# First block of a convolution and SiLU kernel: 32 by 32 tiles of TensorE for the convolution, and a new order of the work around it

## The chip, the cores and the metric

The kernel runs on one core of one Trainium2 chip. Five engines work side by side, each with its own queue in program order: TensorE (PE in the profile; its weight loads are PEld), VectorE (DVE), ScalarE (ACT), GpSimd (POOL) and SyncE (SP), which issues most DMAs. The metric is the device time of one execution in microseconds, the median of several runs; lower is better.

## The reference

```python
def _attn_ref(x, weight):            # x: (8, 4096, 192), weight: (8, 7)
    w = exp(weight - max(weight)) ; w = w / (sum(w) + 1e-9)      # per head, over the 7 taps
    x_pad = concatenate([zeros(6 tokens), x])                    # causal, per sequence
    out[b, s, c] = sum over k of w[head of c, k] * x_pad[b, s + k, c]

def _moe_ref(x, w_in, w_out):        # x: 32768 tokens x 192; w_in: 192 x 2048; w_out: 2048 x 192
    h = x @ w_in
    return (h * (1 / (1 + exp(-h)))) @ w_out
```

A head has 24 channels, so neighbouring channels share their seven taps. `w_in` and `w_out` arrive as 64-bit floats; x, the taps and the result are 32-bit.

## The kernel before, in words

The 32768 tokens go in 32 blocks of 1024 (`TT`), in two halves of 512 (`TB`). Blocks 1 to 31 follow a long list of tokens (`PLAN`): there x and `w_in` are split into parts that TensorE multiplies in a faster format, with products saved by sums of weights. Block 0 is written out by hand, because everything that the others need must first be made: taps, the 64-bit weights turned into 32 bits, and their split parts. The change touches only block 0 and what stands ahead of it.

**Layout.** x has 192 channels. Channels 0 to 127 stand in `nats[0]` (tokens in partitions, 32 at a time) and after a transpose in `xts[0]` (channels in partitions, six columns of `pad` ahead for the causal halo). Channels 128 to 191 stand in `nats[1]` and `xts[1]`, tokens 0 to 511 in partitions 0 to 63 and tokens 512 to 1023 in partitions 64 to 127. After the convolution the same memory is called `x_first[0]` and `x_first[1]`.

**Start** (lines 206 to 247, 390 to 421). SyncE and ScalarE issue the loads: the logits `wexp`, the first half of x in four DMAs, the first part of `w_in` for j=0, the second half of x, channels 128 to 191 (`load(0, 4..7)`), then the other parts of `w_in`. GpSimd makes `sel` (which head a channel belongs to) and `one_hot`. The softmax of the taps runs on VectorE and ScalarE with 8 partitions, and `spread_taps` multiplies it by `sel` on TensorE so that every channel has its taps. `heat` is a matmul of zeros.

**Convolution of block 0.** For channels 0 to 127, `conv_on_pe` (650) multiplies on TensorE with seven diagonal matrices `diags` of 128 by 128, made by ScalarE (line 695), into one PSUM bank for each half of the tokens; `conv_taken` copies a bank to `x_first[0]`. For channels 128 to 191, `conv` (438) runs seven steps on `xts[1]`: the first on ScalarE, six on VectorE.

**Weights.** `Unit` 2j and 2j+1 turn the two parts of column group j of `w_in` (rows 0 to 127 and rows 128 to 191) into 32-bit floats in `wd`. `exponent` is one VectorE and two GpSimd operations, `sign` one on ScalarE, `mantissa`, `sticky` and `rounded` five on VectorE; `top` is the first split part, on ScalarE; `spread` moves rows of the second part to the other half of the partitions by two DMAs. `work(u)` (615) is a generator in two pieces: the first also begins unit u+1, the second rounds, takes the top part and spreads. Units 8 to 11 do `w_out`.

**First products.** `up_first(j, c0)` (675) computes h for column group j, two chunks c of 128 columns and both token halves: four PSUM banks, four products over 128 channels (`x_first[0]`) and four over 64 (`x_first[1]`), then four SiLUs on ScalarE. Banks are taken from and given back to the list `homes`, which has eight. `woven` (637) lays the pieces of two lists into one program order: the next piece is always from the list whose summed cost so far is the smaller share of its whole. One list is the weights (`rest`, whole 392), the other the first products (whole 432). This order holds on each engine; ScalarE does SiLUs, top parts, signs and split parts from the one queue.

After that block 0 multiplies by `w_out` (`down_plain`), and block 1 begins. `halo_in` (423) brings the last six tokens of one block ahead of the next.

Of the kernel before, what the change touches and what calls it, by code (L numbers as in the profile page):

```python
# [18 lines left out]
def kernel(  # L19
# [166 lines left out]
    nats = [const.tile([P, n, SQ], F32, name=f"nat{i}") for i, n in enumerate((TT // SQ, TB // SQ))]  # L186
    xts = [const.tile([P, pad + n], F32, name=f"xt{i}") for i, n in enumerate((TT, TB))]
    xs = [const.tile([P, 3, n], F32R, name=f"xs{i}") for i, n in enumerate((TT, TB))]
# [16 lines left out]

    HALVES = [slice(0, TB // SQ), slice(TB // SQ, TT // SQ)]
    wexp = const.tile([H, K], F32, name="wexp")
    sync.dma_start(out=wexp, in_=weight)
    for i in (1, 0, 2, 3):
        load(0, i, act if i == 1 else sync, HALVES[0])  # L210

# [5 lines left out]

    sel = const.tile([H, 2, P], F32, name="sel")
    one_hot = g_all[:, 0, 1, 0, 0:P]
    vec.memset(one_hot, 0.0)  # L220
    pool.memset(sel, 1.0)
    for sign, base in ((1, 0), (-1, grp - 1)):
        for view, pattern, first in (
            (sel[:, 0, :], [[sign, P]], 0),
            (sel[:, 1, :].rearrange("p (a c) -> p a c", a=2), [[0, 2], [sign, R]], P),
        ):
            pool.affine_select(
                out=view,
                in_=view,
                compare_op=ALU.is_ge,  # L230
                fill=0.0,
                base=base + sign * first,
                pattern=pattern,
                channel_multiplier=-sign * grp,
            )
    pool.affine_select(
        out=one_hot,
        in_=one_hot,
        compare_op=ALU.not_equal,
        fill=1.0,  # L240
        base=0,
        pattern=[[-1, P]],
        channel_multiplier=1,
    )
    pool.memset(xts[0][:, 0:pad], 0.0)
    pool.memset(xts[1][0:R, 0:pad], 0.0)
# [46 lines left out]
    class Unit:  # L293


        def __init__(self, index, key, part):
            j = key[1]
            self.key, self.part, self.j = key, part, j
            lo, hi = {0: (0, CA), 1: (CA, WC), None: (0, WC)}[part]
# [19 lines left out]
        def exponent(self):  # L319
            vec.tensor_single_scalar(self.ex, self.hi, 0x7FF * ONE, op=ALU.bitwise_and)  # L320
            pool.tensor_scalar(
                self.ex, self.ex, scalar1=float(896 * ONE), scalar2=float(1151 * ONE), op0=ALU.max, op1=ALU.min
            )
            pool.tensor_scalar(
                self.ex, self.ex, scalar1=float(896 * ONE), scalar2=8.0, op0=ALU.subtract, op1=ALU.mult
            )
# [51 lines left out]
    def heat(times):  # L378
        for _ in range(times):
            pin(  # L380
                nc.tensor.matmul(
                    banks[7][:, 0 : 2 * P],
                    zeros,
                    zeros.unsqueeze(1).to_broadcast([P, 2, P]),
                    start=True,
                    stop=True,
                )
            )
# [8 lines left out]
    wred = const.tile([H, 3], F32, name="wred")  # L397
# [4 lines left out]
    act.activation(warm, warm, AF.Silu)  # L402
    vec.tensor_scalar(total, total, scalar1=1e-9, scalar2=None, op0=ALU.add)
    vec.reciprocal(part_, total)
    vec.tensor_scalar(wexp, wexp, scalar1=part_, scalar2=None, op0=ALU.mult)

    def spread_taps(k):
        to = banks[6][:, K * k : K * k + K]
        pin(nc.tensor.matmul(to, sel[:, k, :], wexp, start=True, stop=True))

    def take_taps(k):
        vec.tensor_copy(taps[:, k, :], banks[6][:, K * k : K * k + K])

    spread_taps(0)
    heat(1)
    take_taps(0)

    def turn_in(b, k, cols=slice(0, None)):
        vec.transpose(xts[k][:, pad:][:, cols], flat(nats[k])[:, cols])

    turn_in(0, 0, slice(0, TB))
# [193 lines left out]
    def work(u):  # L615

        now = units[u]
        if u:
            begin(u + 1)
        now.mantissa()  # L620
        now.sticky()
        if 2 * NJ < u + 1 < len(units):
            units[u + 1].sign()
        yield
        if not u:
            begin(1)
        now.rounded()
        if u == 1:
            conv_taken(1)
        if now.part is not None:  # L630
            now.top()
# [15 lines left out]

    diags = flat(g_all[:, 0, 6])[:, 0 : K * P].rearrange("p (i c) -> p i c", c=P)

    def conv_on_pe(n):  # L650
        for i in range(K):
            mm(banks[n], diags[:, i, :], xts[0][:, n * TB + i : n * TB + i + TB], i == 0)
            if n == i == 0:
                spread_taps(1)
        homes.append(homes.pop(0))

    def conv_taken(n):
        act.copy(x_first[0][:, ts(n, TB)], banks[n])

# [44 lines left out]
    next(first_[0])  # L704
    turn_in(0, 1)
# [105 lines left out]
```

## Time and profile before

| | |
|---|---|
| median of 3 runs | 2232.61 us (2232.59 to 2232.68) |
| the profiled execution | 2231.81 us, its span 2230.1 us |
| busy in the span | PE 2220.2, DVE 1823.2, ACT 1289.9, POOL 60.9 us |
| products of block 0 by `w_in` | from 18.14 to 62.78 us |
| product of block 0 by `w_out` | 41.4 us from 62.78 us |

Rows of a timeline are: start and length in us, engine, line, operation, what is written and read, partitions by elements and their type, how many are merged (x7), and in brackets the idle time before them and what ended it. L142 and L461 are helpers through which most instructions go, so rows are told apart by the names: `ps` is PSUM, `nat`, `xt`, `g`, `wd`, `w_a`, `w_b`, `fin` and `taps` are the tiles above. A 32-bit matmul shows as two records. 128*128 ahead of the shape is rows by columns of the array that are in use. In groups, the numbers are total busy us, mean ns of one, and idle us before them.

### The profile page before, as it was taken

The numbers are of one execution on the slowest core, as the hardware profiler recorded it, in microseconds if no ns is written. First come the engines' busy times: TensorE is split into PE (matmuls) and PEld (weight loads), VectorE is DVE, ScalarE is ACT, GpSimd is POOL, SyncE is SP. The second block draws the span as 40 slices with busy tenths as digits, with TensorE's granted clock in tenths as the row PEclk, the third lists the DMA queues.
The fourth block names the chain that finished last, engine by engine and source line by source line (L and its number), as shares of the span: only waits on it lengthen the run. The fifth ranks groups of instructions, "written<-read, shape, count | busy, mean of one in ns | idle before, by whom it ended". The sixth has DMA issues, their size and how long they took to land.

```text
span 2230.1 us, 46938 instructions
## 1 busy us (share of the span) xinstructions
PE 2220.2 (100%) x19208; PEld 1638.6 (73%) x19208; DVE 1823.2 (82%) x3017; ACT 1289.9 (58%) x2646; POOL 60.9 (3%) x74
## 2 busy tenths in 40 slices
PE   9999999999999999999999999999999999999998
PEld 4377777777777777777777777777777777777776
DVE  8797888877888878888778887788887788877867
ACT  5266655567555676555665556765466654567543
POOL 6300000000000000000000000000000000000000
PEclk9999999999999999999999999999999999999999
DMA  6301011111011110111110111101111001111001
GB/s 147 61 16 30 11 20 30 30 30 24 7 30 30 30 29 8 23 30 30 30 20 11 29 30 30 30 8 23 30 30 30 16 14 30 30 30 30 5 12 30
DMA packets 408105, 61.75 MB, mean 28 GB/s; under 512 B 402257, under 2 KB 406353, under 8 KB 407889
## 3 DMA queue, kind: packets, MB, share of 16 engines
q1 hardware_dynamic: 404160, 58.30, 15.2%
q8 instruction: 150, 2.46, 0.5%
q10 hardware_dynamic: 3728, 0.46, 0.1%
q14 instruction: 67, 0.54, 0.1%
HBM read 31.46 MB, written 25.17 MB: 25 GB/s over the span
## 4 chain that ended last, share of the span: by engine, by line
PE 98%; DVE 1%; DMA 0%; POOL 0%; issue 0%; SPq 0%; ACT 0%
PE ps L461 98%; DMA g<-in_moe_w_in_dram 0%; DVE nat L142 0%; DVE g L142 0%; POOL g L142 0%; SPq L142 0%; DVE wd L142 0%; DMA out_dram<-fin 0%; DVE fin L142 0%; ACT nat L142 0%; DVE dot L142 0%; ACT fin L142 0%; ACT ps L142 0%; DVE taps L142 0%
## 5 line engine op out<-in xcount | busy, mean ns | idle before, releaser
L461 PE MATMUL ps<-g,wd 128*64 128x256 f32 (+1 forms) x10112 | 1125.6, 384 | 0.0
L461 PEld LDWEIGHTS ps<-g,wd 128*64 128x64 f32 x10112 | 720.4, 137 | 395.7 <-issue 33.7
L142 DVE TENSOR_TENSOR g<-g 128x1024 f32<-128x1024 f32 x806 | 951.2, 1218 | 9.1 <-PE ps L461 5.4
L461 PE MATMUL ps<-xs,w_a 64*128 64x512 f32 x5952 | 852.5, 390 | 1.3 <-DVE dot L142 0.9
L142 ACT ACTIVATE ps<-ps 128x512 f32<-128x512 f32 (+1 forms) x1085 | 568.0, 581 | 298.3 <-PE ps L461 250.5
L461 PEld LDWEIGHTS ps<-xs,w_a 64*128 64x128 f32 x5952 | 601.3, 184 | 103.3 <-DVE dot L142 15.2
L142 ACT ACTIVATE g<-ps 128x512 f32<-128x512 f32 x1024 | 560.1, 615 | 51.5 <-PE ps L461 43.8
L461 PE MATMUL ps<-xs,w_b 64*128 64x512 f32 x2976 | 506.6, 391 | 0.0
L142 DVE COPY dot<-ps 128x1 f32<-128x1 f32 x992 | 155.4, 157 | 353.8 <-PE ps L461 344.6
L142 DVE SCALAR_TENSOR_TENSOR nat<-xt,taps,nat 128x512 f32<-128x512 f32 (+1 forms) x378 | 373.5, 1001 | 3.0 <-ACT nat L142 2.5
L461 PEld LDWEIGHTS ps<-xs,w_b 64*128 64x128 f32 x2976 | 309.2, 184 | 50.5 <-issue 11.5
L142 ACT COPY fin<-ps 128x256 f32<-128x256 f32 (+1 forms) x127 | 47.7, 376 | 408.0 <-PE ps L461 408.0
L142 DVE TENSOR_TENSOR fin<-fin,ps 128x256 f32<-128x256 f32 x248 | 95.7, 404 | 17.2 <-PE ps L461 17.2
L142 DVE STREAM_TRANSPOSE fin<-fin 128x256 f32<-128x256 f32 (+1 forms) x189 | 83.3, 441 | 4.6 <-ACT fin L142 3.1
L142 ACT ACTIVATE nat<-xt,taps 128x512 f32<-128x512 f32 (+1 forms) x63 | 58.6, 933 | 16.1 <-DVE xt L142 14.7
L142 DVE STREAM_TRANSPOSE xt<-nat 128x1024 f32<-128x1024 f32 (+1 forms) x65 | 61.9, 953 | 5.3 <-DMA nat<-in_x_dram 5.3
L142 DVE TENSOR_TENSOR xs<-nat,xs 128x1024 fp32r<-128x1024 f32 (+1 forms) x62 | 59.0, 951 | 0.0
L142 DVE SCALAR_TENSOR_TENSOR xs<-xs 128x1024 fp32r<-128x1024 f32 (+1 forms) x62 | 58.9, 950 | 0.1
L142 ACT ACTIVATE xs<-nat 128x1024 fp32r<-128x1024 f32 (+1 forms) x62 | 52.5, 846 | 10.9 <-DVE nat L142 10.9
L142 ACT ACTIVATE fin<-ps 128x256 f32<-128x256 f32 x93 | 35.8, 385 | 39.5 <-PE ps L461 38.1
L142 POOL TENSOR_SCALAR g<-g 128x512 int32<-128x512 int32 (+2 forms) x24 | 52.0, 2166 | 17.3 <-DVE g L142 10.1
L142 ACT COPY xt<-xt 64x6 f32<-64x6 f32 x56 | 10.9, 195 | 69.0 <-DVE xt L142 68.4
(55 smaller groups left out, 260.2 us busy)
## 6 DMA issues: line engine op xcount, KB each, us to landing
out_dram<-fin SPq DMA_DIRECT2D x242, 96.0 KB, 2.7
nat<-in_x_dram SPq DMA_DIRECT2D x124, 128.0 KB, 3.0
nat<-in_x_dram SPq DMA_DIRECT2D x135, 64.0 KB, 2.6
g<-in_moe_w_out_dram SPq DMA_DIRECT2D x4, 384.0 KB, 3.5
w_b<-w_b SPq DMA_DIRECT2D x8, 192.0 KB, 4.4
fin<-in_moe_w_out_dram SPq DMA_DIRECT2D x4, 384.0 KB, 4.1
g<-in_moe_w_in_dram SPq DMA_DIRECT2D x2, 512.0 KB, 5.3
fin<-in_moe_w_in_dram SPq DMA_DIRECT2D x2, 512.0 KB, 7.5
```

The source lines that it names most:

```text
L142: return lambda *args, **kw: pin(getattr(self.engine, name)(*args, **kw))
L461: return pin(nc.tensor.matmul(to, lhs, rhs, start=start, stop=True, skip_group_check=True))
```

## The change

- x of channels 0 to 127 is loaded by quarters of 256 tokens, a quarter in each 32 partitions, four DMAs with rows of 512 bytes for all 1024 tokens. Four transposes give `x_q`: partition 32q+c holds channel 32g+c of quarter q. Three ScalarE copies bring the halos. The tile is the old `xts[0]` with some columns more.
- The taps come in the new layout from one product with 48 partitions (`sel_q`, `mask`, `spread_logits`) straight in PSUM (`taps_all`); VectorE alone makes the diagonals from there, in two operations, 32 by 32 each.
- `conv_on_pe` issues 7 x 4 x 4 products of 32 by 32 with 256 columns; group g writes partitions 32g, quarter q bank q. Four copies take them out. It runs once, not once for each half.
- The second transpose of x and the second call of the convolution go, with the wait between them.
- Unit 0's exponent is made on VectorE, and it is rounded ahead of the transpose of channels 128 to 191.
- For j=0, `up_both` replaces two `up_first`: eight banks, all eight products over 128 channels first, then those over 64 channels by pairs of chunks, with the SiLUs of each pair. Its pieces cost 72, 18, 18 instead of 36, 18, 18, 36.
- For block 1, the halo is copied by four ScalarE copies instead of one of GpSimd.

```diff
+    x_q = const.tile([P, GQ, pad + TQ], F32, name="xt0")
+    xts = [flat(x_q)[:, 0 : pad + TT], const.tile([P, pad + TB], F32, name="xt1")]
...
-    for i in (1, 0, 2, 3):
-        load(0, i, act if i == 1 else sync, HALVES[0])
+    wexp = const.tile([HG, K], F32, name="wexp")
+    sync.dma_start(out=wexp, in_=weight.unsqueeze(0).to_broadcast([NG, H, K]))
+    for q in range(4):
+        src = x.flatten_outer_dims()[q * TQ : q * TQ + TQ, 0:P].rearrange("(k t) c -> t k c", t=SQ)
+        to = flat(nats[0])[SQ * q : SQ * q + SQ].rearrange("p (k c) -> p k c", c=P)
+        (act if q % 2 else sync).dma_start(out=to, in_=src)
...
         def exponent(self):
             vec.tensor_single_scalar(self.ex, self.hi, 0x7FF * ONE, op=ALU.bitwise_and)
-            pool.tensor_scalar(
+            engine = pool if self.late else vec
+            engine.tensor_scalar(
...
     load_in(0, 0, sync)
-    for i in range(4):
-        load(0, i, sync, HALVES[1])
     for i in range(4, 8):
         load(0, i, sync)
...
+    pin(nc.tensor.matmul(banks[6][:, 0 : GQ * K], flat(sel_q), flat(spread_logits), start=True, stop=True))
+    for k in (1, 0):
+        of = flat(sel[:, 4 * k : 4 * k + 4, :])
+        pin(nc.tensor.matmul(banks[7][:, K * k : K * k + K], of, w_norm, start=True, stop=True))
     heat(1)
-    take_taps(0)
+    def turn_q(g):
+        for g_ in (g, g + 1):
+            vec.transpose(x_q[:, g_, pad:], nat_q[:, :, g_, :])
...
+            elif b == 1:
+                for g in range(GQ):
+                    act.copy(xts[0][SQ * g : SQ * g + SQ, 0:pad], x_q[P - SQ : P, g, TQ : TQ + pad])
...
-    def conv_on_pe(n):
-        for i in range(K):
-            mm(banks[n], diags[:, i, :], xts[0][:, n * TB + i : n * TB + i + TB], i == 0)
+    def conv_on_pe():
+        for i in reversed(range(K)):
+            for g in range(GQ):
+                for q in range(4):
+                    at_ = slice(SQ * q, SQ * q + SQ)
+                    to = banks[q][SQ * g : SQ * g + SQ, 0:TQ]
+                    mm(to, diags[at_, i, g, :], x_q[at_, g, i : i + TQ], i == K - 1)
+        homes.extend([homes.pop(0) for q in range(4)])
+
+    def conv_taken(q):
+        act.copy(x_first[0][:, ts(q, TQ)], banks[q][:, 0:TQ])
...
+    def up_both(j):
+        to = {(c, n): homes.pop(0) for n in range(2) for c in range(4)}
+        for (c, n), bank in to.items():
+            mm(bank, w_in[0][:, j, c, :], x_first[0][:, ts(n, TB)], True)
+        yield
+        for c0 in (0, 2):
+            for c in (c0, c0 + 1):
+                for n in range(2):
+                    w = rows(w_in[1], n)[:, j, (c + 2 * n) % 4, :]
+                    mm(to[c, n], w, rows(x_first[1], n))
+            for c in (c0, c0 + 1):
+                for n in range(2):
+                    act.activation(g_slot(j, c, n), to[c, n], AF.Silu)
+                    homes.append(to[c, n])
+            yield
...
-    for i in range(K):
-        act.activation(diags[:, i, :], one_hot, AF.Copy, scale=taps[:, 0, i : i + 1])
+    for q in range(1, 4):
+        act.copy(x_q[SQ * q : SQ * q + SQ, :, 0:pad], x_q[SQ * q - SQ : SQ * q, :, TQ : TQ + pad])
+    diagonals(slice(K - 2, K))
+    diagonals(slice(0, K - 2))
...
-    conv_on_pe(0)
+    conv_on_pe()
     begin(0)
     first_ = [work(u) for u in range(2)]
-    take_taps(1)
-    turn_in(0, 0, slice(TB, TT))
     next(first_[0])
+    next(first_[0])
+    for k in range(2):
+        vec.tensor_copy(taps[:, k, :], banks[7][:, K * k : K * k + K])
+    for q in range(4):
+        conv_taken(q)
+    units[0].top()
     turn_in(0, 1)
     halo_in(0, 2)
     conv(0, 1, 0)
-    conv_taken(0)
-    conv_on_pe(1)
-    conv(0, 1, 1)
-    next(first_[0])
     next(first_[1])
-    for i in range(2, 5):
+    for i in range(1, 4):
         conv(0, 1, i)
     next(first_[1], None)
-    for i in range(5, K):
+    for i in range(4, K):
         conv(0, 1, i)
...
-    woven(rest, [f for j in range(NJ) for c in (0, 2) for f in pieces(up_first(j, c), 36 - 9 * c, 18 + 9 * c)])
+    ups = pieces(up_both(0), 72, 18, 18)
+    ups += [f for j in range(1, NJ) for c in (0, 2) for f in pieces(up_first(j, c), 36 - 9 * c, 18 + 9 * c)]
+    woven(rest, ups)
```

More of the change, by code (lines that the diff above doesn't have):

```diff
@@ L216 @@
     act.activation(warm, warm, AF.Exp)
-    sel = const.tile([H, 2, P], F32, name="sel")
-    one_hot = g_all[:, 0, 1, 0, 0:P]
-    vec.memset(one_hot, 0.0)
[L221 to L245, printed above, removed]
+    sel = const.tile([HG, NG + 2, SQ], F32, name="sel")
+    sel_q = const.tile([HG, 4, SQ], F32, name="selq")
+    mask = const.tile([HG, GQ], F32, name="mask")
+    one_hot = const.tile([P, SQ], F32, name="hot")
+    pool.memset(sel, 1.0)
+    pool.memset(mask, 1.0)
+    vec.memset(one_hot, 0.0)
+    for sign in (1, -1):
+        pool.affine_select(
+            out=sel[:, 0:NG],
+            in_=sel[:, 0:NG],
+            compare_op=ALU.is_ge,
+            fill=0.0,
+            base=0 if sign > 0 else grp - 1,
+            pattern=[[sign * (SQ + H * grp), NG], [sign, SQ]],
+            channel_multiplier=-sign * grp,
+        )
+    for sign in (1, -1):
+        pool.affine_select(
+            out=mask,
+            in_=mask,
+            compare_op=ALU.is_ge,
+            fill=0.0,
+            base=0 if sign > 0 else H - 1,
+            pattern=[[-sign * H, GQ]],
+            channel_multiplier=sign,
+        )
+    for q in range(4):
+        pool.affine_select(
+            out=one_hot,
+            in_=one_hot,
+            compare_op=ALU.not_equal,
+            fill=1.0,
+            base=-SQ * q,
+            pattern=[[-1, SQ]],
+            channel_multiplier=1,
+        )
+    pool.memset(x_q[0:SQ, :, 0:pad], 0.0)
     pool.memset(xts[1][0:R, 0:pad], 0.0)
@@ L297, in __init__ @@
             j = key[1]
-            self.key, self.part, self.j = key, part, j
+            self.key, self.part, self.j, self.late = key, part, j, index > 0
             lo, hi = {0: (0, CA), 1: (CA, WC), None: (0, WC)}[part]
@@ L381, in heat @@
                 nc.tensor.matmul(
-                    banks[7][:, 0 : 2 * P],
+                    banks[5][:, 0 : 2 * P],
                     zeros,
@@ L402, with turn_in @@
     act.activation(warm, warm, AF.Silu)
+    vec.tensor_reduce(sel_q[:, 0, :], sel[:, 0:GQ, :].rearrange("r g c -> r c g"), axis=AX.X, op=ALU.add)
+    vec.tensor_copy(sel_q[:, 1:4, :], sel_q[:, 0, :].unsqueeze(1).to_broadcast([HG, 3, SQ]))
+    vec.tensor_copy(sel[:, NG : NG + 2, :], sel[:, NG - 2 : NG, :])
     vec.tensor_scalar(total, total, scalar1=1e-9, scalar2=None, op0=ALU.add)
     vec.reciprocal(part_, total)
[L405 to L414, printed above, removed]
-    heat(1)
-    take_taps(0)
-    def turn_in(b, k, cols=slice(0, None)):
-        vec.transpose(xts[k][:, pad:][:, cols], flat(nats[k])[:, cols])
-    turn_in(0, 0, slice(0, TB))
+    vec.scalar_tensor_tensor(
+        out=spread_logits,
+        in0=wexp.unsqueeze(1).to_broadcast([HG, GQ, K]),
+        scalar=part_,
+        in1=mask.unsqueeze(2).to_broadcast([HG, GQ, K]),
+        op0=ALU.mult,
+        op1=ALU.mult,
+    )
+    vec.tensor_scalar(w_norm, wexp, scalar1=part_, scalar2=None, op0=ALU.mult)
+    pin(nc.tensor.matmul(banks[6][:, 0 : GQ * K], flat(sel_q), flat(spread_logits), start=True, stop=True))
+    for k in (1, 0):
+        of = flat(sel[:, 4 * k : 4 * k + 4, :])
+        pin(nc.tensor.matmul(banks[7][:, K * k : K * k + K], of, w_norm, start=True, stop=True))
+    heat(1)
+    def turn_q(g):
+        for g_ in (g, g + 1):
+            vec.transpose(x_q[:, g_, pad:], nat_q[:, :, g_, :])
+    def turn_in(b, k):
+        vec.transpose(xts[k][:, pad:], flat(nats[k]))
+    turn_q(0)
+    turn_q(2)
     def halo_in(b, i):
@@ L627, in work @@
         now.rounded()
-        if u == 1:
-            conv_taken(1)
         if now.part is not None:
-            now.top()
+            if u:
+                now.top()
             now.spread(w_in[1][:, now.j, :, :])
```

32 lines of the change are left out of this document (20 added, 12 removed).

## The prediction

> **What bounds the kernel now.** I read the chain of waits first, and in it only where it changes engine for good:
>
> ```profile
> 22.87 0.04 issue
> 22.91 79.62 PE ps L461 x303
> ...
> 120.67 2071.66 PE ps L461 x18360
> ```
>
> From 22.91 us the end hangs on TensorE (PE), but for short hops between 102.5 and 120.7. So the change can gain only before 22.91 or by the work that TensorE still has to do after it. Then TensorE in order of time:
>
> ```profile
> 1.12 2.93 PE L381 MATMUL ps<-zeros 128*128 128x256 f32 x6 [1.12 <-DVE warm L142]
> 16.42 1.88 PE L461 MATMUL ps<-xt,g 128*128 128x512 f32 x4
> 18.14 3.60 PE L461 MATMUL ps<-nat,wd 128*128 128x512 f32 x8
> 22.91 9.56 PE L461 MATMUL ps<-nat,wd 64*128 64x512 f32 x28 [1.18 <-DVE nat L142]
> 30.60 1.88 PE L461 MATMUL ps<-nat,wd 128*128 128x512 f32 x4
> 62.78 41.42 PE L461 MATMUL ps<-g,wd 128*64 128x512 f32 x192
> ```
>
> and its groups in the first 125 us:
>
> ```profile
> L461 PE MATMUL ps<-nat,wd 64*128 64x512 f32 x64 | 15.3, 602 | 1.2 <-DVE nat L142 1.2
> L461 PE MATMUL ps<-xt,g 128*128 128x512 f32 x28 | 12.5, 598 | 0.5 <-ACT g L142 0.5
> ```
>
> Every f32 product is two records. One of 512 columns takes 0.43 us of the array (12.5/28); the 64-row ones run two at once (15.3/64 is half that). The convolution of channels 0 to 127 holds the array from 5.54 to 18.14. Then come, for each j, an upper part (16 records, 6.9 us) and a lower part (16 records in pairs, 3.4 us). Half of j=0's upper part runs at 18.14; then TensorE waits 1.18 us for VectorE (DVE), which convolves channels 128 to 191. The upper part of j=1 starts at 30.60 (the row's start).
>
> VectorE is dense from 13.24 on:
>
> ```profile
> 4.68 0.71 DVE L142 STREAM_TRANSPOSE xt<-nat 128x512 f32<-128x512 f32 x1
> 7.83 0.43 DVE L142 TENSOR_SCALAR g<-g 128x512 int32<-128x512 int32 x1 [2.44 <-DMA g<-in_moe_w_in_dram]
> 9.56 0.39 DVE L142 TENSOR_SCALAR g<-g 128x512 int32<-128x512 int32 x1
> 9.87 0.68 DVE L142 SCALAR_TENSOR_TENSOR g<-g 128x512 int32<-128x512 int32 x1
> 13.24 0.75 DVE L142 SCALAR_TENSOR_TENSOR nat<-xt,taps,nat 128x512 f32<-128x512 f32 x1 [1.06 <-ACT nat L142]
> 14.11 1.49 DVE L142 SCALAR_TENSOR_TENSOR g<-g 128x512 f32<-128x512 int32 x2
> 15.63 0.69 DVE L142 SCALAR_TENSOR_TENSOR wd<-g 128x512 f32<-128x512 f32 x1
> 19.79 1.17 DVE L142 SCALAR_TENSOR_TENSOR g<-g 128x256 f32<-128x256 int32 x2
> 21.33 1.53 DVE L142 SCALAR_TENSOR_TENSOR nat<-xt,taps,nat 128x512 f32<-128x512 f32 x2
> 26.37 0.69 DVE L142 TENSOR_TENSOR g<-wd,w_a 128x512 f32<-128x512 f32 x1
> 29.80 0.42 DVE L142 SCALAR_TENSOR_TENSOR wd<-g 128x256 f32<-128x256 f32 x1
> 30.15 0.42 DVE L142 TENSOR_TENSOR g<-wd,w_b 128x256 f32<-128x256 f32 x1
> ```
>
> Weights of unit 0 are ready at 16.32 (15.63+0.69), of unit 3 (j=1, second part) at 30.22.
>
> **The change part by part.** *Start.* These rows set it:
>
> ```profile
> 0.81 0.40 ACTq L142 DMA_DIRECT2D nat<-in_x_dram  x1
> 1.18 1.04 POOL L142 TENSOR_SCALAR_AFFINE_SELECT sel<-sel 8x128 f32<-8x128 f32 x4
> 2.65 0.28 ACT L142 ACTIVATE wexp<-wexp,wred 8x7 f32<-8x7 f32 x1
> 1.27 1.40 SPq L142 DMA_DIRECT2D nat<-in_x_dram  x3
> 2.72 5.09 DMA g<-in_moe_w_in_dram
> 3.98 0.47 PE L409 MATMUL ps<-wexp,sel 8*128 8x7 f32 x2
> 8.34 4.08 POOL L142 TENSOR_SCALAR g<-g 128x512 int32<-128x512 int32 x2 [5.79 <-DVE taps L142]
> ```
>
> A second x transfer on ScalarE's queue moves what follows there by 0.4 us, so the exponential (2.65) and the taps: in PSUM at 4.9 instead of 4.45. The wait for x hides that; uncovered it costs 0.4. GpSimd now has eight selects where four took 1.04; with its fills it is done by 3.5, hidden too. The four x transfers are issued by 2.1 instead of 2.67, but carry 512 KB instead of 256 KB before the first transpose. I bound their landing by 4.1 (issue alone counts: 4.68-0.5) and 6.7 (the 2 us between the first issue's landing and 4.68 doubled), and take 4.6, near the first, since rows of 512 B replace rows of 128 B. Four transposes of 256 columns (0.71 for 512, less overlap: 0.37 each) end at 6.1. The diagonals, 2.15 us of ScalarE until now, cost VectorE 0.36 (256 elements, 0.42 by the 30.15 row) and 0.82 (640, from 0.42 and 0.69): to 7.3.
>
> *First weights.* Their DMA moves up by one issue slot, 0.5, so from 7.81 to 7.3, when VectorE is just free. Three dependent operations of 0.43 replace the one and GpSimd's 4.08. From 7.3 VectorE does: exponent 1.3, mantissa and sticky 0.95, taps 0.2, a transpose 0.65, plus what stood between 13.24 and 22.86 (9.63: six convolution steps, two roundings, two exponent starts). That is 12.7, so the last convolution step ends at 20.0. If GpSimd disturbs less (the pair at 19.79 took 1.17 where two of 0.42 were due), it is 0.6 less; if the second part of the weights or the first ScalarE step is late, some 0.4 more. I take 12.6: 19.9 against 22.86, **3.0 us earlier** (bounds 2.4 to 3.7 with x at 4.6). Nothing in the VectorE order after that is changed, so unit 3 is ready at 27.2 instead of 30.22.
>
> *The convolution.* 112 products of 32x32 with 256 columns, 224 records of 0.215. If all 16 tiles run at once, a tap takes 0.43 and seven 3.0; if only two do, as in any row here, 224x0.215/2 = 24.1. The groups above show row halves side by side and the 62.78 row column halves (192 records in 41.4: 0.216 each), so tiles are independent in both directions; I take 3.5, near the lower end. It runs from 6.6 to 10.1. Four ScalarE copies make x usable at 11.4, before unit 0's weights at 12.0. Behind the copies on ScalarE's queue stand the first top part, the halo and the first step of the other convolution (0.54+0.27+0.72), which VectorE needs at 13.7: the convolution may end at 10.9 unnoticed, and **each us beyond that delays everything 1:1**.
>
> *TensorE after it.* All of j=0's upper part runs from 12.0 to 18.9, its lower part from 19.95 to 23.5. Now the point where I differ from a plain sum of savings. The order of ScalarE is woven by the costs given to the pieces. The rows of before show it:
>
> ```profile
> 26.49 0.63 ACT L142 ACTIVATE w_a<-wd 128x512 fp32r<-128x512 f32 x1 [4.29 <-DVE wd L142]
> 27.02 2.04 ACT L142 ACTIVATE g<-ps 128x512 f32<-128x512 f32 x4
> 28.93 0.65 ACT L142 ACTIVATE w_a<-g 128x512 fp32r<-128x512 f32 x1
> 29.62 0.68 ACT L142 ACTIVATE g<-fin 128x512 int32<-128x512 uint8 x1
> 30.27 0.42 ACT L142 ACTIVATE w_b<-wd 128x256 fp32r<-128x256 f32 x1
> 30.59 2.04 ACT L142 ACTIVATE g<-ps 128x512 f32<-128x512 f32 x4
> ```
>
> The first four SiLUs come behind unit 2's top part (26.49), the next four behind unit 3's (30.27). With all of j=0's upper part as one piece of cost 72 of 432, the weights' stream runs on while its share (65/392 = 0.1658) is under 72/432 = 0.1667, so unit 3's second piece goes ahead of *all* SiLUs. They wait for 27.2+0.32, and j=0 now holds all eight banks. The first bank is free after a SiLU of 0.58, so j=1's upper part starts at 28.2, not at 23.5: TensorE stands still for 4.7 us. Against 30.60 the gain is **2.4 us**. What follows keeps its cover: unit 3's other rows go by DMA,
>
> ```profile
> 21.44 1.15 SPq L142 DMA_DIRECT2D wd<-wd  x2
> 23.43 0.29 PEld L461 LDWEIGHTS ps<-nat,wd 64*128 64x128 f32 x3 [0.22 <-DMA wd<-wd]
> ```
>
> about 2.0 to 2.6 after the weights, so at 29.8, and are needed at 31.7; later units are 3.0 earlier while TensorE is 2.4 earlier. The four ScalarE halo copies for block 1 instead of one by GpSimd (4x0.19) lie in a stretch where ScalarE idles:
>
> ```profile
> 76.73 0.19 ACT L142 COPY xt<-xt 64x6 f32<-64x6 f32 x1 [8.22 <-DVE xt L142]
> ```
>
> Sum: the profiled span of 2230.1 becomes 2227.7. The profiled execution took 2231.81 and the median of the runs is 2232.61; the same 2.4 off the median gives **2230.2**.
>
> One rule of the Trainium skill speaks against the 3.5: page "TensorE: Matmul & The Clock Gate", section "Wait — 56ns, not 53.3ns?", has matmul starts never closer than about 25 ns. By it, 224 starts would be 5.6 us, an estimate, and the result 1.3 us later. The same page of the Trainium skill, section "Measured speedup vs the span model", gives 16 such tiles 10.6 times the speed of one. No run here shows either.
>
> **The rivals.**
>
> *Banks are not the limit after all* (SiLUs get in earlier, or VectorE's chain is shorter). Then j=1's lower part waits for the DMA at 29.8 instead of starting, as now, at 34.1 (30.60 plus 3.44). That gives 4.3 to 4.8: 2227.8 to 2228.3, less if x lands at 4.1. For it: only 0.001 in the share of pieces decides the order. Against: the same comparison is what put the 30.27 row ahead of the 30.59 row.
>
> *The clock drops in the new gap.* Six matmuls of 256 columns took 2.93 us at the start, 0.43 apart; later 512 columns take 0.43. TensorE thus starts at half speed for some 2.9 us, although the granted clock reads 1.00 there. If 4.7 us without work bring that back, half of 2.9 is lost: 2231.6. For it: the longest TensorE wait quoted above is 1.18 us, so nothing shows that the array stays warm. Against: 4.7 may be too short. By the Trainium skill, page "TensorE: Matmul & The Clock Gate", section "What's actually happening", a whole idle window of some 3.4 us, free-running, throttles the array; a gap of 4.7 need not hold one.
>
> *Column groups take turns* (the other side). If only the four row groups run at once, a tap takes 4x0.43 and the convolution 12.0, as long as now. It ends at 18.6, 7.7 beyond the slack: 2237.9. The point from which it decides: over 6.7 us nothing is gained. For it: no row shows more than two tiles at once. Against: both directions overlap in the rows above. At two at once (24.1) it would be 2250.
>
> **How the numbers follow.** What a measurement of this kernel can tell from no change is about 0.2%, 4.5 us: faster means under 2228.1, slower over 2237.1. Forecast (gain of 1.3 to 3.5: 2229.1 to 2231.3): 0.39. Clock: 0.13. Banks free earlier or a shorter chain: 0.27, all counted as faster though its centre lies at the bound, since an earlier x would add to it. Column groups in turn, or slower still: 0.15. A convolution of 5 to 9 us: 0.06, 2231 to 2235. So faster 0.27, same 0.58, slower 0.15. The range goes from 2226.8 (4.8 and x 0.5 earlier, with half a us for GpSimd) to 2235.0; it leaves out most of the slow case and a little below.
>
> **What would show it.** The seven taps as 224 records within about 3.5 us from 6.6; the last convolution step on VectorE ending near 19.9; the top part of unit 3 near 27.2, directly ahead of eight SiLUs; a TensorE wait of over 4 us on ScalarE ahead of j=1's upper part, which starts near 28.2; records of 0.43 there and not 0.86; the down product starting near 60.4 instead of 62.78. The forecast is wrong if the convolution lasts over 4.3 us, if x or the first weights land after 7.3, or if that wait is not there.

## The result and the profile after

| kernel | median us | lowest to highest |
|---|---|---|
| before (18 runs) | 2232.85 | 2232.25 to 2235.06 |
| changed (18 runs) | 2237.11 | 2234.58 to 2238.71 |

The ratio is 1.0017, with an interval of 1.001 to 1.0025: slower by 4.3 us, about 0.2%, where 2.4 us of gain were forecast. The profiled execution took 2236.91 us, its span is 2235.2. Executions of the changed kernel differ by up to 4.1 us. Only one of them was traced, so what makes them differ is not shown.

TensorE in order of time, of the changed kernel:

```profile
7.67 6.60 PE L494 MATMUL ps<-xt,g 32*32 32x256 f32 x209
16.11 0.66 PE L494 MATMUL ps<-xt,g 32*32 32x256 f32 x15 [1.84 <-issue]
17.52 7.13 PE L494 MATMUL ps<-nat,wd 128*128 128x512 f32 x16 [0.74 <-ACT nat L142]
25.36 3.77 PE L494 MATMUL ps<-nat,wd 64*128 64x512 f32 x16 [0.70 <-DVE nat L142]
33.79 33.74 PE L494 MATMUL ps<-nat,wd 128*128 128x512 f32 x96 [4.66 <-ACT g L142]
67.47 2.79 PE L494 MATMUL ps<-g,wd 128*64 128x512 f32 x12
```

The 224 records of the convolution are in two rows: 209 of them, 1.84 us without work that no engine explains ("issue"), and the last 15. The convolution ends at 16.77 (16.11 + 0.66), not at 10.1. The upper part of j = 1 starts at 33.79 (before 30.60, forecast 28.2), behind a standstill of 4.66 us. The product by `w_out` starts at 67.47 instead of 62.78, 4.69 later. So the whole loss has arisen by there: 3.19 of it by 33.79, the other 1.5 between 33.79 and 67.47.

VectorE and ScalarE, of the changed kernel:

```profile
5.26 1.42 DVE L142 STREAM_TRANSPOSE xt<-nat 128x256 f32<-128x256 f32 x4
...
8.80 1.35 DVE L142 TENSOR_SCALAR g<-g 128x512 int32<-128x512 int32 x3 [1.08 <-DMA g<-in_moe_w_in_dram]
...
19.61 2.33 DVE L142 SCALAR_TENSOR_TENSOR nat<-xt,taps,nat 128x512 f32<-128x512 f32 x3 [3.20 <-ACT nat L142]
22.98 2.32 DVE L142 SCALAR_TENSOR_TENSOR nat<-xt,taps,nat 128x512 f32<-128x512 f32 x3
...
32.38 0.42 DVE L142 SCALAR_TENSOR_TENSOR wd<-g 128x256 f32<-128x256 f32 x1
```

```profile
16.82 1.20 ACT L142 COPY nat<-ps 128x256 f32<-128x256 f32 x4 [5.04 <-PE ps L494]
...
18.85 0.73 ACT L142 ACTIVATE nat<-xt,taps 128x512 f32<-128x512 f32 x1
...
32.84 0.42 ACT L142 ACTIVATE w_b<-wd 128x256 fp32r<-128x256 f32 x1 [1.84 <-DVE wd L142]
33.16 2.04 ACT L142 ACTIVATE g<-ps 128x512 f32<-128x512 f32 x4
```

VectorE begins the weights at 8.80 instead of 7.3 and then idles 3.20 us at 19.61. It waits there for the first step of the other convolution, which stands on ScalarE (18.85) behind the four copies (16.82), which wait for TensorE. The last convolution step ends at 25.30, 2.44 later than before (22.86). Unit 3 is ready at 32.80, and its top part (32.84) goes directly ahead of the SiLUs (33.16), as forecast.

### The profile page after: what moved, and what is told of

Its sections match the earlier page's. It is cut to its first block, busy times and chain, and to the rows that moved or that the text cites. A ratio compares the mean times of both kernels' runs of the same rounds, so it can differ in the third digit from the quotient of the medians.

```text
span 2235.2 us, 47341 instructions
## 1 busy us (share of the span) xinstructions
PE 2218.2 (99%) x19406; PEld 1632.6 (73%) x19406; DVE 1826.7 (82%) x3029; ACT 1292.0 (58%) x2648; POOL 50.6 (2%) x73
## 3 DMA queue, kind: packets, MB, share of 16 engines
q8 instruction: 151, 2.47, 0.5%
## 4 chain that ended last, share of the span: by engine, by line
PE 98%; DVE 1%; ACT 0%; issue 0%; ACTq 0%
PE ps L494 98%; DVE g L142 0%; DVE nat L142 0%; DVE wd L142 0%; DVE fin L142 0%; ACT nat L142 0%; DVE dot L142 0%; DVE w_a L142 0%; ACT ps L142 0%; ACT fin L142 0%; ACT w_a L142 0%; ACT g L142 0%; ACT w_b L142 0%; ACT xt L142 0%; ACTq L142 0%
## 5 line engine op out<-in xcount | busy, mean ns | idle before, releaser
L494 PEld LDWEIGHTS ps<-xs,w_a 64*128 64x128 f32 x5952 | 592.6, 184 | 108.6 <-DVE dot L142 14.8
L494 PE MATMUL ps<-xs,w_b 64*128 64x512 f32 x2976 | 501.0, 391 | 0.0
L494 PEld LDWEIGHTS ps<-xs,w_b 64*128 64x128 f32 x2976 | 302.3, 184 | 53.0 <-issue 11.5
L142 DVE STREAM_TRANSPOSE xt<-nat 128x1024 f32<-128x1024 f32 (+2 forms) x67 | 62.0, 930 | 2.6 <-DMA nat<-in_x_dram 2.5
L142 ACT ACTIVATE xs<-nat 128x1024 fp32r<-128x1024 f32 (+1 forms) x62 | 52.5, 847 | 10.9 <-DVE nat L142 10.9
L494 PE MATMUL ps<-nat,wd 128*128 128x512 f32 (+1 forms) x128 | 44.7, 613 | 6.1 <-ACT g L142 4.7
L142 ACT COPY xt<-xt 64x6 f32<-64x6 f32 (+2 forms) x63 | 12.4, 197 | 64.5 <-DVE xt L142 63.7
```

Of the source, the lines that this page charges most:

```text
L142: return lambda *args, **kw: pin(getattr(self.engine, name)(*args, **kw))
L494: return pin(nc.tensor.matmul(to, lhs, rhs, start=start, stop=True, skip_group_check=True))
```

## The experiments

Three questions were open: whether the standstill and ScalarE's order are two separate terms, why the convolution took 9.1 us (7.67 to 16.77), and what the drop of the clock costs. Two theories were set against each other: that the loss came in through ScalarE's queue and the woven order, behind a late convolution; or that TensorE's own queue or the transfers set the times and neither order costs anything. All runs, with the kernel before on the same chip beside them:

| kernel | median us | before us | ratio (interval) |
|---|---|---|---|
| e1_order | 2233.63 | 2233.22 | 1.0 (0.999 to 1.001) |
| e2_heat | 2236.28 | 2233.22 | 1.001 (1.0001 to 1.0019) |
| e3_six | 2234.71 | 2233.22 | 1.0005 (0.9996 to 1.0014) |
| e4_wexp | 2239.35 | 2233.22 | 1.0026 (1.0016 to 1.0035) |
| e5_both | 2229.2 | 2232.34 | 0.9986 (0.9977 to 0.9995) |
| e6_scalar | 2232.28 | 2232.34 | 0.9999 (0.999 to 1.0008) |
| e7_noheat | 2228.96 | 2232.34 | 0.9985 (0.9976 to 0.9994) |
| e8_quarter | 2230.4 | 2232.34 | 0.9991 (0.9982 to 0.9999) |
| e9_weights | 2235.32 | 2232.45 | 1.001 (1.0001 to 1.0019) |
| e10_quarter | 2230.13 | 2232.45 | 0.999 (0.9981 to 0.9999) |
| e11_all | 2233.78 | 2232.45 | 1.0006 (0.9997 to 1.0015) |

**The woven order (e1_order).**

```diff
-    ups = pieces(up_both(0), 72, 18, 18)
+    ups = pieces(up_both(0), 71, 19, 18)
```

> One number changes: the pieces of the first group cost 71, 19, 18 instead of 72, 18, 18, so that the first four SiLUs come ahead of unit 3's top part on ScalarE instead of behind it. Theory (bank wait): the 4.66 us in which TensorE waits for ScalarE ahead of j=1's upper part shrink to under 0.5, that part starts by 29.1 instead of 33.79, its first records start 0.43 apart instead of 0.86, and what is left of the wait (for unit 3's rows, ready at 32.8 plus 2.4 for the DMA) comes ahead of j=1's lower part, at most 3 us long. Sum: 3.4 us less than the changed kernel, about 2233.7. Rival (the gap is only moved, the end hangs on VectorE's weights): less than 1 us gained, about 2236.5.

TensorE of this kernel:

```profile
16.82 1.10 PE L494 MATMUL ps<-xt,g 32*32 32x256 f32 x15 [2.31 <-issue]
18.67 13.03 PE L494 MATMUL ps<-nat,wd 128*128 128x512 f32 x32 [0.75 <-ACT nat L142]
32.65 32.36 PE L494 MATMUL ps<-nat,wd 128*128 128x512 f32 x96 [0.95 <-ACT g L142]
64.94 5.37 PE L494 MATMUL ps<-g,wd 128*64 128x512 f32 x24
```

A row of a timeline merges shapes. By shape, the 32 records are the upper and the lower part of j = 0, 16 each, and the 96 are j = 1 to 3 (the expectations of later runs call them the lower products of j = 0). Below are the group of the lower part from 17 to 33.5 us, the row of the windows from 16.4 to 23.2 us (granted clock 0.50) and the first SiLUs on ScalarE:

```profile
L494 PE MATMUL ps<-nat,wd 64*128 64x512 f32 x16 | 3.7, 602 | 0.0
```

```profile
16.40:23.20 6.80, 5.63 (x21) 2.16 (x22) 2.38 (x4) 3.19 (x8) 2.48 (x2) 0.50 0.53 133
```

```profile
32.01 2.05 ACT L142 ACTIVATE g<-ps 128x512 f32<-128x512 f32 x4
```

The standstill is 0.95 instead of 4.66, but part of that difference is no gain: in this execution the clock fell ahead of the 32 records, which take 13.03 us where e5_both needs 10.77, so TensorE comes to its wait later. The upper part of j = 1 starts at 32.65, 1.14 earlier than in the changed kernel, though the convolution ends 1.15 later (17.92 for 16.77). So the order is worth 2.3 us against the end of the convolution: the SiLUs no longer wait for unit 3's top part, which comes at 33.96. They still stand on ScalarE behind unit 2's pieces, so the start expected by 29.1 was missed by 3.5 us. From there to `w_out` it takes 32.29 (64.94 - 32.65) instead of 33.68 (67.47 - 33.79), since the clock does not fall again. The median is as expected (2233.7): 0.4 above the kernel before instead of 4.3.

**More warming (e2_heat).**

```diff
-    heat(3)
+    heat(4)
...
-    heat(1)
+    heat(2)
```

> One product of zeros more ahead of the taps and one more ahead of the convolution. Theory (the array is at half speed while it convolves, because too little ran on it before): the records of one tile in the convolution start 0.22 us apart instead of 0.43, and the convolution ends 2 to 3 us earlier than 16.8; the time falls by as much, to 2234 to 2235. Rival (the feeding of small matmuls sets their distance): still 0.43 apart, and the time stays or grows by the added products, 2237 to 2238.

```profile
8.75 5.04 PE L494 MATMUL ps<-xt,g 32*32 32x256 f32 x205
15.73 0.68 PE L494 MATMUL ps<-xt,g 32*32 32x256 f32 x19 [1.94 <-issue]
...
33.41 34.06 PE L494 MATMUL ps<-nat,wd 128*128 128x512 f32 x96 [3.81 <-ACT g L142]
```

The records go faster (205 in 5.04 instead of 209 in 6.60), but they begin 1.1 later, and the pause still comes: the convolution ends at 16.41, 0.36 earlier than in the changed kernel. The pause has moved four records forward (205 instead of 209) for two more zero products, eight instructions: a sign that it hangs on a count of instructions. A standstill of 3.81 still costs the clock: 34.06 us for the 96 records where e1_order needs 32.36. Neither expectation is met (2234 to 2235, or 2237 to 2238). Nor do the added products explain the faster records: the granted clock, as the packed traces record it, rises at 10.31 us here and at 12.72 in the changed kernel, but at 10.43 in e6_scalar, with the same zero products as the changed kernel, and at 10.73 in e7_noheat, with none.

**Six taps instead of seven (e3_six).** Tap 0 of channels 0 to 127 is left out.

```diff
-        for i in reversed(range(K)):
+        for i in reversed(range(1, K)):
```

> The convolution on TensorE leaves out tap 0, so that block 0's channels 0 to 127 lack one of seven terms: 192 records instead of 224. Theory (the 1.84 us without work after record 209 is a wait for the next chunk of TensorE's instructions, which comes by DMA after so many instructions): no such pause within the convolution, the chunk is fetched while long matmuls run, and the convolution ends at 13.2 to 13.5 instead of 16.8; the time falls by 3.2, to about 2233.9. Rival (the pause belongs to the tiles: it stands ahead of the last tap, or its last products wait for a semaphore): a pause of 1.5 to 2 us stays ahead of the end of the convolution, and only about 0.5 us is gained: 2236.6.

```profile
7.59 5.84 PE L494 MATMUL ps<-xt,g 32*32 32x256 f32 x192
...
30.59 35.03 PE L494 MATMUL ps<-nat,wd 128*128 128x512 f32 x96 [4.60 <-ACT g L142]
65.55 4.94 PE L494 MATMUL ps<-g,wd 128*64 128x512 f32 x22
```

With 192 records there is no pause, and the upper part of j = 1 is 3.2 earlier (30.59 against 33.79), which is 1:1 with the end of the convolution (13.43 against 16.77). The standstill is the same 4.60. The median gained only 2.4, not the expected 3.2: behind the standstill the half clock lasted longer here, 34.96 us up to `w_out` where the changed kernel took 33.68.

**The logits on GpSimd's queue (e4_wexp).**

```diff
-    sync.dma_start(out=wexp, in_=weight.unsqueeze(0).to_broadcast([NG, H, K]))
+    pool.dma_start(out=wexp, in_=weight.unsqueeze(0).to_broadcast([NG, H, K]))
```

> The load of the logits in 48 partitions goes by GpSimd's queue instead of SyncE's. Theory (its issue of 0.96 us on SyncE instead of 0.41 holds back x and the first weights): the first x transfer of SyncE is issued at 0.8 instead of 1.8, x lands by 4.7 instead of 5.1, the first weights by 8.0 instead of 8.8, and the time falls by 0.4 to 0.8. Rival (x and weights are bound by the bytes in flight): they land within 0.2 of before, and the time is within 0.3 of 2237.1.

```profile
5.63 0.15 DVE L142 TENSOR_REDUCE wred<-wexp 48x1 f32<-48x7 f32 x1 [4.51 <-DMA wexp<-in_weight_dram]
```

A miss: the idea was to free SP's first slot, and the first weights do land earlier (7.78 instead of 8.78), but the logits reach VectorE at 5.63 instead of 3.68. The convolution then starts at 9.27 and all behind it is later.

**ScalarE's order, with and without the woven order (e5_both, e6_scalar).** In both, the second convolution's halo and first step stand ahead of the copies; e5_both has the costs 71, 19, 18 too.

```diff
-    for q in range(4):
-        conv_taken(q)
-    units[0].top()
     turn_in(0, 1)
     halo_in(0, 2)
     conv(0, 1, 0)
+    for q in range(4):
+        conv_taken(q)
+    units[0].top()
```

> The changed kernel with the new ScalarE order alone. Theory: VectorE from 16.4 us on is 3.2 us earlier, unit 3 ready near 29.6, the products of j = 1 start near 30.6 instead of 33.79 behind a standstill of about 2.2 us instead of 4.66. If the clock falls only in a longer standstill, the records behind it are at full clock and the time is 2237.1 - 3.2 - 1.5 = 2232.4 us; if it falls in this one too, 2233.9. Rival (ScalarE's order costs nothing, since the woven order sets the start): 2237.1, the standstill unchanged.

> The woven order of e1_order, and on ScalarE the second convolution's halo copy and first step ahead of the four copies of the first convolution and of unit 0's top part. Theory (ScalarE's order is the second term: the second convolution waits on ScalarE behind the copies, which wait for TensorE): VectorE's first step of the second convolution starts at about 16.4 us, right behind the sign steps, instead of 19.61, its last step ends near 22.1, unit 3 is ready near 29.6 and the lower products of j = 0 start near 30.5, as soon as the 32 upper products are through, without a wait; the products behind them end 2.1 earlier than in e1_order: 2231.5 us, ahead of the kernel before by 1.3 to 2. Rival (what VectorE gains is hidden by TensorE's own queue, which starts no earlier): the time of e1_order, 2233.6.

e6_scalar, VectorE and then TensorE:

```profile
15.63 2.54 DVE L142 SCALAR_TENSOR_TENSOR nat<-xt,taps,nat 128x512 f32<-128x512 f32 x3
...
19.22 2.32 DVE L142 SCALAR_TENSOR_TENSOR nat<-xt,taps,nat 128x512 f32<-128x512 f32 x3
...
28.60 0.42 DVE L142 SCALAR_TENSOR_TENSOR wd<-g 128x256 f32<-128x256 f32 x1
```

```profile
16.78 0.72 PE L494 MATMUL ps<-xt,g 32*32 32x256 f32 x15 [3.25 <-issue]
18.20 45.97 PE L494 MATMUL ps<-nat,wd 128*128 128x512 f32 x128 [0.70 <-ACT nat L142]
```

The convolution ends even later (17.50), but VectorE no longer hangs on it: its steps start at 15.63 without a wait and end at 21.54 (25.30 in the changed kernel), and unit 3 is ready at 29.02 instead of 32.80. So VectorE's 1:1 delay came through ScalarE's queue. The time of 2232.28 meets the expected 2232.4, yet not quite by the expected way: in this execution the half clock fell on the products of j = 0, which ran on so long that no standstill was left. The windows of this kernel show it from 20 to 27 us (after the span each engine's busy time, then the granted clock, 0.71):

```profile
20.00:27.00 7.00, 7.00 (x13) 3.02 (x12) 6.86 (x13) 2.10 (x5) 2.76 (x3) 0.71 0.45 141
```

e5_both:

```profile
7.32 6.37 PE L494 MATMUL ps<-xt,g 32*32 32x256 f32 x224 [0.31 <-DVE g L142]
15.75 10.77 PE L494 MATMUL ps<-nat,wd 128*128 128x512 f32 x32 [2.06 <-ACT nat L142]
28.02 32.36 PE L494 MATMUL ps<-nat,wd 128*128 128x512 f32 x96 [1.50 <-ACT g L142]
60.31 10.09 PE L494 MATMUL ps<-g,wd 128*64 128x512 f32 x46
```

Better than expected (2231.5): the product by `w_out` starts at 60.31, 2.47 earlier than in the kernel before. In this execution the convolution had no pause. The median is 3.1 under that of the kernel before. Measured against it, the change loses 4.26; with the woven order alone that is 0.41, with ScalarE's alone -0.06, with both -3.14. So they take away 3.8, 4.3 and 7.4: two terms that nearly add. (The row of 96 records is j = 1 to 3; the expectation of 30.5 stands for it.)

**The pause (e7_noheat).** e5_both without the calls `heat(3)` and `heat(1)`.

```diff
-    heat(3)
...
-    heat(1)
```

> e5_both without the four warming products of zeros (two instructions for each of their two passes, 16 in all). Theory (the pause in the convolution comes after a fixed number of TensorE instructions, since the next ones are fetched then): the pause comes 8 records later, behind record 217 instead of 209, with 7 records behind it, and lasts about 2 us all the same; the time stays within 0.5 us of e5_both. Rival (the pause belongs to a place in the convolution or to a time): behind record 209 again, or at 13.9 us whatever the record. The warming theory: without them the convolution starts at half clock as it does in the changed kernel, 0.43 us between a tile's records, so nothing is lost.

```profile
7.50 5.91 PE L492 MATMUL ps<-xt,g 32*32 32x256 f32 x217 [0.33 <-DVE g L142]
15.11 0.63 PE L492 MATMUL ps<-xt,g 32*32 32x256 f32 x7 [1.70 <-issue]
...
27.62 32.36 PE L492 MATMUL ps<-nat,wd 128*128 128x512 f32 x96 [0.61 <-ACT g L142]
```

The pause stands behind record 217, exactly eight later: the count of instructions decides where it comes. Without the zero products nothing is lost: 217 records take 5.91 us, and the medians are 0.2 apart. When it ends goes with a transfer of instructions. The instruction queue's line in windows of half a us, of the changed kernel from 13.5, of e7_noheat from 12.5 and of e5_both from 10 us; each has one packet of 0.02 MB, and the share is of the window:

```profile
q8 instruction: 1, 0.02, 15.5%
```

```profile
q8 instruction: 1, 0.02, 12.7%
```

```profile
q8 instruction: 1, 0.02, 20.6%
```

In the first two TensorE went on at 16.11 and 15.11, 2.6 us behind the start of the packet. In all ten profiled kernels with a pause that distance is 2.5 to 3.0 us, whether the packet starts at 12.4 or at 17.4. In e5_both the packet went at 10, long before record 209, and there was no pause. That the pause is the wait for the next instructions is therefore shown by place and by time, though the trace does not name the engine that a packet is for; what decides when the packet goes is not shown.

**Quarters first (e8_quarter on e5_both, e10_quarter on e7_noheat).**

```diff
-            for g in range(GQ):
-                for q in range(4):
+            for q in range(4):
+                for g in range(GQ):
```

> e5_both with the two inner loops of the convolution on TensorE exchanged, so that a quarter's four products of a tap are issued one behind the other. Theory: the tiles still run side by side (the 209 records in 6.6 us or less), and at the pause the first two quarters are complete, so that ScalarE copies them within it; the upper products then wait for two copies less and start some 0.5 to 0.7 us earlier: 2230.9 us. Rival 1 (a quarter's copy is released only by the last product): the start of e5_both, 2231.5. Rival 2 (products of one row group behind each other take turns): the convolution takes up to four times its 6.6 us, and the kernel is slower by more than 5 us.

> e7_noheat with the two inner loops of the convolution exchanged as in e8_quarter: two or three quarters are copied before the pause ends, so ScalarE's copies end up to 0.6 us earlier, and the upper products start up to 0.6 earlier. Theory (VectorE's chain up to unit 3 sets the start of the lower products, so TensorE's earlier start goes into its wait there): the time of e7_noheat within 0.4 us, 2229.0, the wait ahead of the 96 records longer by what the upper products gained. Rival (TensorE's own queue is the limit): 2228.4.

ScalarE of e8_quarter, and the first products of e10_quarter:

```profile
15.02 0.62 ACT L142 COPY nat<-ps 128x256 f32<-128x256 f32 x2
15.93 0.65 ACT L142 COPY nat<-ps 128x256 f32<-128x256 f32 x2 [0.29 <-PE ps L494]
```

```profile
15.51 10.79 PE L492 MATMUL ps<-nat,wd 128*128 128x512 f32 x32
27.53 32.36 PE L492 MATMUL ps<-nat,wd 128*128 128x512 f32 x96 [1.23 <-ACT g L142]
```

In e8_quarter two copies go ahead from within the pause (14.38 to 15.24), and the 209 records take 6.49 us, so the tiles still run side by side. What that gains is read from e10_quarter against e7_noheat, which both have a pause of 1.70: the upper products start 0.73 earlier (15.51 against 16.24), but the 96 records only 0.09 (27.53 against 27.62), since VectorE's chain sets them: the wait ahead of them grows from 0.61 to 1.23. The medians, 2230.4 and 2230.13, are 1.2 above those without the edit. So the way was as expected and the time of e10_quarter was not (2229.0 within 0.4); the profiled executions, 2228.67 and 2228.96, are the fastest of their kernels and do not show why.

**The first weights earlier (e9_weights on e7_noheat, e11_all on e10_quarter).** ScalarE issues them right behind its two x transfers.

```diff
+    words_ = flat(g_all[:, 1, 0:2]).bitcast(I32)[:, 0 : 8 * P].rearrange("p (a e c) -> p a e c", a=2, e=2)
+    from_ = moe_w_in.bitcast(I32)[0:P].rearrange("p (a m c) -> p a m c", a=2, c=2 * P)
+    act.dma_start(out=words_, in_=from_[:, :, 0:2, :])
...
-    load_in(0, 0, sync)
```

> e7_noheat with the first weights' transfer issued from ScalarE's queue right behind its two x transfers, about 1.73 us, instead of from SP's at 2.75. Theory (the first weights were late because of their issue slot): they land near 7.8 instead of 8.4 to 8.8, where VectorE has just ended the diagonals, so its weight work starts at once and everything up to unit 3 is 0.3 to 1.0 us earlier: the lower products of j = 0 start near 27.0 instead of 27.62, 2228.4 us. ScalarE's table load and exponential begin 0.7 later, which the wait for the logits covers. Rival (the data itself is late, whatever its issue: the channel of x and weights is full): they land at 8.4 or later and nothing is gained, 2229.0.

> e9_weights and e10_quarter together: if VectorE's start is the limit and the two shifts add where they meet, the lower products start near 27.0 with a wait under 0.6 ahead of them: 2228.3 us. Rival (neither matters): 2229.0.

VectorE and TensorE of e9_weights:

```profile
8.02 1.42 DVE L142 STREAM_TRANSPOSE xt<-nat 128x256 f32<-128x256 f32 x4 [2.41 <-DMA nat<-in_x_dram]
10.40 1.67 DVE L142 TENSOR_SCALAR g<-g 128x512 int32<-128x512 int32 x4
```

```profile
19.93 1.07 PE L494 MATMUL ps<-xt,g 32*32 32x256 f32 x7 [4.34 <-issue]
```

Its last quarter of x, issued at 2.28, with KB and us to landing:

```profile
nat<-in_x_dram SPq DMA_DIRECT2D x1, 128.0 KB, 5.6
```

Both are slower than even the rival had it (2229.0). The weights do land early, as the theory had it (7.52 and 7.88 for 7.8). But the last quarter of x, issued half a us behind them, now lands behind them too: at 7.90 in e9_weights, where e7_noheat, which issues it ahead of the weights, has it at 5.24. The transposes start at 8.02 instead of 5.73, and everything else hangs on x. In this execution the pause grew to 4.34 as well; in that of e11_all (2231.02, the fastest of its kernel) it was 1.87.

## Why the prediction was wrong

- **The convolution is the step that failed.** "I take 3.5, near the lower end. It runs from 6.6 to 10.1." The mechanism was right: all 16 tiles run side by side. Its start, the clock, the spacing of the records and the supply of instructions were wrong or left out. A view of the changed kernel cut at 7.78 us shows the first 16 records begun within 0.11 us, and one of the instructions on that line from 7.6 to 9 and from 12.9 to 14 us shows how long one takes (shortest, median, longest in ns):

```profile
7.67 0.73 PE L494 MATMUL ps<-xt,g 32*32 32x256 f32 x16
```

```profile
L494 PE MATMUL ps<-xt,g x49: 626/629/631, 7.7 to 9.0; 32*32 32x256 f32 x49
```

```profile
L494 PE MATMUL ps<-xt,g x59: 372/396/528, 12.4 to 13.9; 32*32 32x256 f32 x59
```

  So no column group takes turns, but TensorE ran at half clock for two thirds of the records. Of the 6.67 us by which the convolution ended late, 1.07 are its start (7.67 for 6.6), 3.33 its first 209 records (6.60 where 209/224 of 3.5 is 3.27), 1.84 the pause, and 0.43 the last 15 (0.66 for 0.23). The start is late because the transposes begin at 5.26 instead of 4.6: the last quarter of x lands at 5.14, and VectorE works on the taps up to 5.23, since the logits come at 3.68 (2.18 in the kernel before). The pause was in no term and no rival. The half clock stood in the prediction as a rival for the later gap; that the *first* products can run in it, as the zero products of before do, was not carried over. Of the rule of the Trainium skill that was weighed, page "TensorE: Matmul & The Clock Gate", section "Wait — 56ns, not 53.3ns?" (starts never closer than 25 ns), the runs show the contrary: 16 starts within 0.11 us, and at full clock in e2_heat 137 records begun from 10.7 to 13.3 us, 19 ns apart. That is still slower than the 13 ns which 0.215 us for 16 tiles supposes, so 3.5 would have been short at full clock too (224 x 19 ns is 4.3). By that spacing, an estimate, 209 records take 4.0 us, so of the 3.33 some 2.6 are the half clock.
- **The first weights and x.** "From 7.81 to 7.3" was wrong: they were waited for until 8.80. The row of before could not show it, but the SP rows of after do:

```profile
0.81 0.96 SPq L142 DMA_DIRECT2D wexp<-in_weight_dram  x1
2.75 0.68 SPq L142 DMA_DIRECT2D g<-in_moe_w_in_dram  x1
```

  The logits for 48 partitions take SP 0.96 us, which eats up the slot that was saved: the first weights are issued at 2.75, as before at 2.72, and land a us later than before. That x, now twice as large, holds them up is argued, not shown by itself; e9_weights shows the reverse, x landing behind weights issued ahead of it. In e6_scalar, where VectorE does not wait for the convolution, the last convolution step ends at 21.54 instead of the forecast 19.9, so the term of 3.0 was really 1.3. Of the 1.64 that are missing, 1.35 are the first weights (8.65 there for 7.3): VectorE's own work, 12.6, was nearly right.
- **The 1:1 rule was right.** "The convolution may end at 10.9 unnoticed, and each us beyond that delays everything 1:1." It ended 5.9 beyond it; the last convolution step came 5.4 late (25.30 for 19.9), j = 1's upper part 5.6 late (33.79 for 28.2). e6_scalar removed it by ScalarE's order.
- **The standstill was right**: 4.66 for 4.7, behind unit 3's top part and with all eight banks held. e1_order shows the cause: with the SiLUs ahead of that top part, the start moves by 2.3 against the convolution's end.
- **The clock's rival came true.** 33.68 us from j = 1 to `w_out` where before took 32.18: 1.5, forecast 1.45, with a chance of 0.13. The mechanism was right, the size lucky: after the 4.60 us of e3_six the same loss was 2.8 (34.96 for 32.18). The windows of the changed kernel from 33.2 to 36.6 us, granted clock 0.50:

```profile
33.20:36.60 3.40, 2.81 (x4) 1.25 (x5) 3.33 (x7) 3.40 (x9) 3.24 (x3) 0.50 0.15 39
```

  The cited 3.4 us of the Trainium skill, page "TensorE: Matmul & The Clock Gate", section "What's actually happening", agrees in its length, and no pause starts it anew: in the 13 packed traces every change of the granted clock lies a whole number of steps of 3.41 us behind the first one recorded (changed kernel: 12.72, 33.20, 36.61). That the whole step must be idle does not hold here: behind the pauses of 1.94 to 3.25 us in e1_order, e2_heat, e4_wexp and e6_scalar the clock fell as well.
- **The sum closes.** 2230.2 + 5.6 for the late start + 1.5 for the clock is 2237.3; 2237.11 was measured. The rival with column groups in turn gave 2237.9 and was near by chance alone: its mechanism is refuted. The range ended at 2235.0 because a convolution of 9.1 us had been given little chance. Two of the prediction's own signs of being wrong came, the convolution over 4.3 us and the first weights after 7.3.
- **Banks as the limit.** The rival without the bank limit gave 2227.8 to 2228.3. e7_noheat, with a standstill of 0.61 only and without the ScalarE wait, came to 2228.96. So the change's own gain is there once both orders are set right, 3.4 us under the kernel before; e5_both and e7_noheat beat both kernels, and between these two nothing is decided.

## What to carry to other kernels

A fast step that feeds an in-order engine must be followed through that engine's queue: ask for each instruction behind its consumer whether it would rather go first, since a slip in the fast step then reaches only those that need it. Early work, and work behind a gap, is costed at the half clock at which its first records can run, and hundreds of tiny products need their instructions in time. Before a row of merged records is given a name, its shapes are looked at. Where two streams are woven by shares, look at ties: here 72 or 71 decided 3.8 us.

## What was not expected of the hardware

- TensorE stood still 0.87 to 4.34 us in the midst of ready work, at a record number that moved with the count of TensorE instructions ahead (205, 209, 217 for 8 more, 0 and 16 fewer), until 2.5 to 3.0 us after the start of a packet of instructions. Not settled: why the packet goes at 10 us in one execution and at 13.5 in another.
- Four zero products and the small tap products did not lift the clock: records still took 629 ns at 9 us. Windows that end before 12.72 us show a granted clock of 1.00 in the changed kernel, but its packed trace has no record of the clock before 12.72, so that 1.00 (and the one ahead of 4.2 us in the kernel before) is not a measurement. In e5_both the records begin at 4.32, and this row of its windows, from 7.8 to 11.1 us, reads 0.50 where its tiles take 629 ns:

```profile
7.80:11.10 3.30, 3.30 (x123) 2.60 (x102) 2.47 (x7) 0.75 (x2) 0.00 (x0) 0.50 0.62 142
```

- What makes the clock fall was read from the same steps of 3.41 us. Behind the start, each of the eight steps that ended in a fall left TensorE without work for 1.88 to 3.41 us; the steps with 1.84 us or less (the changed kernel's pause among them) did not, nor did one with 1.97 in e4_wexp. So where a pause lies in the steps decides as well as its length. What load counts as work is open (in e5_both the clock fell behind 1.55 us without work and small products beside it), and with one trace for each kernel so is how much of the spread of the runs comes from this.
